# Carrying a running phase from chunk to chunk by one row, and storing a row of decays turned: linear attention with an FFN on one Trainium2 core

## The chip, the cores and the metric

One NeuronCore of a Trainium2 chip runs the whole program. The metric is the device time of one execution in microseconds. Times of one kernel mostly agree within 1%; a run over 1.5% above the fastest of its kernel is called slow and left out of every comparison. Medians and ranges below count all runs of a kernel, slow ones too; ratios use fast runs alone. The kernel before takes 300.9 us (median of four runs, 299.94 to 301.81).

The profiles name the engines in short. PE is TensorE, which multiplies matrices, and PEld its weight loads; DVE is VectorE, ACT ScalarE, POOL GpSimd. SP or SPq is SyncE, which issues most of the DMAs. PSUM is the memory into which PE writes its products. The granted clock is the share of full speed at which PE was let run. A line of waits, such as `a <- b: 57.8, 9, 18.1`, says that `a` waited for `b` for 57.8 us in all, 9 times, at the longest 18.1 us.

## The reference, cut to what matters

```python
# q, k, v, a_re, a_im: (batch 4, heads 8, seq 768, dim 48), fp32
mag = np.sqrt(a_re * a_re + a_im * a_im)
scale = np.minimum(mag, 0.999) / (mag + 1e-06)
a_re_n, a_im_n = (a_re * scale, a_im * scale)
for t in range(S):                       # complex decay of a 48x48 state per head
    new_re = ar * S_re - ai * S_im
    new_im = ar * S_im + ai * S_re
    S_re, S_im = (new_re + kv, new_im)   # kv = outer(k[t], v[t])
    y[:, :, t] = np.einsum('bhd,bhde->bhe', q[:, :, t], S_re)
# then, on the 3072 x 384 tokens x made of y:
out = sigmoid(x @ w_gate) * (x @ w_val) @ w_out      # d_ff 1536
```

A product of complex decays is a product of sizes and a sum of angles. The kernel cuts each batch's 768 steps into 6 chunks of 128 (24 chunks in all). In a chunk, a triangular matmul turns per-step log sizes into cumulative decays and per-step angles into cumulative phases. Only a phase modulo 2π matters, but it must contain the angles of all the earlier chunks of the same batch. How that carry is made is one subject of the change; the other is how the row of a chunk's total decays is stored.

## The kernel before

Every piece of work is a named step for a chunk `m` or a group `g` of one to three chunks. Lists of numbers, `TIMES`, are sorted to give each engine its fixed order. The parts that matter here:

```python
# total decay of a chunk: row 127 of EE, one row of 384 floats, to DRAM ...
nc.sync.dma_start(scr[b][c:c + 1], T[EE][L - 1:L, 0])                    # step scr
# ... and back as 48 partitions x 8 heads, for the chunks lo..hi of a group
nc.sync.dma_start(rbe[b][p0:p0 + D, lo:hi],
                  scr[b][lo:hi].rearrange("c (h d) -> d c h", d=D))      # step rbe, p0 = 0, 64
# DVE needs it before it can pass the state on
nc.vector.tensor_tensor(out=arr[b][:, c], in0=rbe[b][:, c - 1],
                        in1=rbe[b][:, c], op=ALU.mult)
# [...]
# phase of a chunk, in turns; A[:, 1, s] holds arctan, 128 x 384 fp32
nc.tensor.matmul(ct, wt_t, T[A][:, 1, s], start=True, stop=False)        # step ct
if prev:                                                                 # earlier chunks
    nc.tensor.matmul(ct, on_t, T[prev[0]], start=False, stop=False)      # the ones-matmul
# step run, on POOL: RUN = previous RUN + this chunk's angles
nc.gpsimd.tensor_tensor(out=T[RUN], in0=T[prev[0]], in1=th, op=ALU.add)
# step r16 on DVE rounds ct to an integer, step nid on PE subtracts it:
nc.tensor.matmul(T[CT][:, :HD], nid_t, T[R16], start=False, stop=True)
# step cs on ACT: Abs and two Sin of ct, which give cosine and sine
```

`wt_t` is the triangle over 2π, `on_t` a full matrix of 1/(2π), both fp32.

Of the kernel before, what the change touches and what calls it, by code (L numbers as in the profile page):

```python
# [25 lines left out]

BRISK = 1
# [3 lines left out]
        1.6, 5.95],  # L31
    "wg": [
        9.61, 19.75, 36.31],
    "wv": [
        14.45, 28.31, 41.72],
    "wo": [
        47.02, 54.23, 60.97],
    "la": [
        0.7, 5.05, 11.4, 23.58, 30.23, 40.45, 49.35, 57.89, 62.4, 67.84,
        74.04, 81.04, 87.55, 98.44, 105.44, 109.79, 122.19, 127.84,  # L40
        135.59, 150.82, 155.17, 160.92, 191.36, 199.88],
    "sq": [
        5.05, 16.5, 38.15, 55.66, 73.64, 94.11, 116.4, 140.2, 168.36,
        212.24],
    "add": [
        5.92, 18, 21.03, 39.65, 40.74, 57.78, 58.87, 75.78, 76.87,
        78.36, 96.26, 97.34, 100.63, 119.7, 120.79, 122.39, 142.35,
        147.63, 150.71, 173.29, 174.38, 175.97, 213.75, 214.83],
    "min": [
        6.52, 20.52, 22.74, 42.49, 43, 60.46, 59.95, 79.84, 80.35,  # L50
        80.86, 100.12, 102.74, 101.71, 125.67, 121.87, 126.18, 151.69,
        148.72, 152.2, 176.95, 175.46, 181.85, 215.81, 216.32],
    "lna": [
        7.31, 19.12, 44.34, 60.42, 80.37, 105.13, 129.27, 158.34,
        187.78, 216.56],
    "lnm": [
        6.93, 23.36, 43.64, 61.12, 81.49, 104.12, 128.25, 157.32,
        186.77, 217.26],
    "inv": [
        9.73, 19.99, 48.13, 61.82, 82.88, 106.53, 131.29, 159.73,  # L60
        188.97, 217.95],
    "r": [
        10.76, 23.25, 24.23, 49.97, 48.99, 64.17, 62.69, 86.02, 85.04,
        84.07, 107.71, 108.69, 109.66, 132.48, 133.45, 134.43, 161.89,
        162.87, 160.92, 192.62, 191.13, 190.16, 219.8, 218.82],
    "cl": [
        7.48, 27.36, 24.23, 44.59, 45.88, 61.99, 62.63, 83.42, 84.06,
        85.15, 106.64, 107.28, 108.37, 130.32, 129.68, 131.61, 158.99,
        160.56, 161.2, 188.31, 190.46, 188.95, 218.82, 218.18],
    "ee": [  # L70
        8.97, 28.86, 25.72, 46.09, 47.37, 62.84, 63.6, 84.65, 85.41,
        86.17, 107.92, 108.68, 109.44, 132.31, 130.53, 133.06, 160.75,
        161.51, 162.26, 190.74, 191.5, 189.99, 219.79, 219.03],
    "scr": [
        31.13, 29.78, 26.65, 47.01, 48.3, 64.65, 68.74, 88.45, 88.9,
        87.1, 115.04, 110.69, 114.59, 134.89, 134.44, 133.99, 169.43,
        169.88, 168.98, 192.88, 192.43, 190.91, 220.72, 223.91],
    "rbe": [
        38.2, 35.85, 50.55, 71.34, 80.09, 93.19, 121.29, 120.39, 136.99,
        171.98, 198.06, 195.81, 226.56],  # L80
    "lq": [
        2.95, 12.3, 22.23, 27.8, 39.1, 51.45, 63.3, 72.69, 78.74, 84.49,
        90.74, 96.64, 106.34, 113.24, 119.04, 124.54, 138.34, 144.92,
        151.72, 158.62, 170.33, 175.83, 181.33, 196.71],
    "v16": [
        9.1, 22.23, 27.8, 35.8, 67.46, 63.66, 81.38, 79.33, 88.79,
        91.11, 111.66, 110.64, 116.37, 144.3, 125.16, 146.61, 147.12,
        165.65, 169.45, 172.27, 227.38, 181.33, 186.83, 235.3],
    "qke": [
        9.9, 29.78, 31.58, 55, 50.95, 65.15, 71.29, 86.99, 89.31, 98.32,  # L90
        114.57, 117.9, 123.36, 138.92, 144.81, 135.91, 170.47, 167.64,
        163.85, 193.59, 195.39, 197.2, 223.78, 225.58],
    "atan": [
        11.4, 30.9, 51.06, 65.64, 88.76, 112.41, 136.76, 164.69, 195.44,
        221.84],
    "ct": [
        12.06, 33.89, 37.44, 51.92, 54.71, 66.55, 69.24, 90.06, 92.74,
        94.35, 115.66, 119.6, 121.21, 138.43, 140.37, 144.63, 168.26,
        171.08, 178.77, 198.7, 201.88, 203.65, 222.8, 226.31],
    "run": [  # L100
        18.98, 33.38, 37.08, 53.26, 56.8, 73.09, 91.62, 92.7, 94.23,
        113.59, 117.39, 137.95, 143.32, 149.74, 166.16, 172.78, 199,
        200.2, 203.37, 222.8],
    "r16": [
        13.55, 36.67, 38.93, 53.42, 56.2, 68.05, 70.09, 91.55, 94.88,
        96.54, 117.81, 121.54, 123.53, 141.01, 142.2, 146.64, 169.76,
        172.57, 179.89, 200.2, 203.37, 205.17, 224.29, 227.8],
    "nid": [
        14.16, 37.28, 39.54, 54.02, 56.81, 68.7, 70.93, 92.2, 95.96,
        98.03, 118.53, 122.18, 124.13, 141.65, 143.01, 147.33, 170.92,  # L110
        176.68, 180.79, 201.18, 205.42, 207.04, 225.01, 228.64],
    "cs": [
        14.69, 39.48, 40.75, 54.39, 57.37, 69.46, 71.37, 92.57, 96.98,
        98.52, 118.9, 123.2, 124.74, 142.18, 144.67, 147.7, 171.51,
        177.06, 182.07, 201.55, 206.01, 207.41, 225.38, 229.01],
    "ks": [
        16.13, 40.92, 42.79, 56.91, 60.91, 70.89, 79.74, 94.01, 99.19,
        104.49, 120.34, 126.78, 131.07, 143.61, 150.45, 153.44, 173.04,
        180.35, 184.16, 203.84, 207.83, 217.73, 226.82, 230.45],
    "qs": [  # L120
        17.13, 41.93, 45.62, 58.18, 62.37, 72.09, 80.75, 95.34, 103.29,
        109.17, 122.33, 129.6, 132.5, 145.31, 155.5, 158.59, 177.63,
        181.9, 192.63, 205.63, 211.28, 218.74, 228.27, 235.25],
    "tp": [
        18.14, 19.02, 43.37, 42.93, 48.3, 47.6, 59.19, 61.45, 63.37,
        64.46, 73.86, 73.09, 86.11, 84.7, 97.26, 96.49, 105.22, 107.92,
        111.6, 112.53, 124.64, 123.34, 132.9, 134.23, 136.45, 143.7,
        146.4, 148.03, 160.12, 161.84, 162.77, 163.7, 182.18, 184.51,
        193.49, 185.44, 196.42, 206.11, 210.03, 213.06, 215.55, 219.63,
        220.78, 221.87, 230.84, 231.77, 240.92, 239.29],  # L130
    "qkT": [
        19.23, 21.22, 45.02, 44.42, 49.39, 48.79, 59.84, 63.23, 64.16,
        65.12, 75.08, 74.15, 87.2, 85.36, 97.93, 97.33, 107.49, 108.58,
        112.25, 113.78, 125.29, 123.99, 133.56, 134.88, 137.61, 147.1,
        148.17, 148.76, 160.77, 162.5, 163.43, 165.33, 182.83, 186.11,
        194.14, 187.74, 197.07, 206.77, 210.68, 213.94, 216.21, 220.28,
        223.58, 222.52, 233.02, 232.42, 242.33, 241.74],
    "sc": [
        19.97, 21.96, 47.16, 47.38, 50.78, 54.49, 60.58, 65.45, 65.23,
        72, 75.89, 76.44, 88.13, 87.05, 99.64, 100.19, 110.18, 111.05,  # L140
        114.03, 114.58, 127.03, 126.48, 134.67, 135.74, 142.3, 148.96,
        149.66, 150.37, 164.14, 164.59, 164.37, 173.5, 183.8, 190.24,
        197.35, 193.93, 200.47, 207.74, 212.35, 214.68, 220.56, 224.79,
        229.29, 224.08, 237.88, 240.21, 243.43, 244.14],
    "mst": [
        20.62, 22.61, 47.59, 48.19, 51.81, 54.92, 61.77, 66.88, 66.28,
        72.95, 77.62, 78.22, 88.99, 87.8, 100.07, 101.9, 110.61, 111.48,
        116.2, 115.01, 130.47, 128.54, 135.48, 136.55, 142.73, 149.39,
        151.78, 152.38, 168.4, 167.8, 165.92, 174.37, 185.02, 190.67,
        198.73, 198.14, 201.86, 209.09, 213.34, 215.54, 220.99, 226.06,  # L150
        231.31, 225.46, 238.31, 241.14, 243.86, 244.73],
    "kv": [
        30.6, 49.33, 49.69, 57.92, 68.16, 87.6, 100.73, 102.34, 109.66,
        125.95, 134.9, 151.08, 155.44, 157, 177.38, 191.75, 213.98,
        230.16, 232.21, 237.19],
    "P": [
        31.21, 49.98, 53.88, 60.44, 68.57, 92.02, 102.5, 106.32, 110.07,
        129.14, 136.08, 154.31, 158.13, 160.16, 178.49, 192.16, 216.8,
        231.91, 234.79, 239.38],
    "y": [  # L160
        23.35, 48.93, 56.16, 70.2, 75.17, 79.13, 91.67, 102.88, 113.3,
        117.8, 133.35, 137.55, 151.77, 153.17, 170.03, 179.9, 191.95,
        209.14, 210.96, 217.78, 228.24, 236.3, 242.55, 245.54],
    "y16": [
        26.48, 50.45, 56.99, 70.99, 75.89, 82.5, 92.1, 106.15, 113.91,
        118.41, 133.96, 138.16, 152.18, 153.78, 175.44, 180.51, 194.31,
        209.75, 211.37, 218.65, 230.74, 236.91, 245.44, 254.09],
    "xp": [
        27.03, 51.17, 57.54, 72.55, 76.99, 86.56, 101.27, 112.04,
        115.12, 119.07, 137.38, 140.2, 154.05, 156.14, 175.99, 181.48,  # L170
        208.45, 211.65, 214.9, 219.46, 238.59, 241.85, 249.83, 258.91],
    "xt": [
        27.57, 51.55, 57.92, 73.88, 78.81, 86.93, 105.35, 113.18,
        115.94, 119.44, 138.79, 141.47, 154.77, 157.86, 177.36, 183.89,
        208.82, 212.14, 215.28, 219.84, 239.84, 244.46, 261.67, 261.94],
    "pg": [
# [744 lines left out]
```

## Time and profile before

| | before |
|---|---|
| median time | 300.9 us |
| span of the profiled run, mean granted clock | 300.8 us, 0.977 |
| PE stream, by my sum | 235.8 us |
| PE stalls in the first 80 us / after | 41.4 / 12.9 us |

PE's stream and stalls come from the start-to-start spacings of PE's instructions in the trace. For each shape the shortest usual spacing is its stream; whatever is above it is a stall, half-clock time included. Stream and stalls leave 10.7 us before the first and after the last matmul.

### The profile page before, as it was taken

What the parts mean: (1) busy time and instruction counts of PE and PEld (TensorE: products, weight loads), DVE (VectorE), ACT (ScalarE), POOL (GpSimd) and SP (SyncE); (2) the same over time, 40 slices, a digit from 0 to 9 for tenths busy, and PEclk for the clock granted to TensorE, in tenths of its full rate; (3) what the DMA queues carried; (4) which work ended last, traced back from release to release, by engine and by line L of the source; (5) the groups of instructions that cost most, each with busy time, mean ns of one, the idle gap of its engine ahead of it and who ended that gap; (6) DMA issues with size and microseconds to landing.
All of it is one profiled execution on the core that took longest, in us unless ns stands there. A gap on an engine that the chain in (4) does not pass through costs nothing.

```text
span 300.8 us, 6265 instructions
## 1 busy us (share of the span) xinstructions
PE 258.9 (86%) x2328; PEld 177.2 (59%) x2328; DVE 212.2 (71%) x389; ACT 208.9 (69%) x368; POOL 161.9 (54%) x173
## 2 busy tenths in 40 slices
PE   0443668649999998998999999999999999999995
PEld 0131446436675675866766666566667666766683
DVE  3251268978993699879889976994699889825340
ACT  3663777838978988978996798579668963334341
POOL 0327684966466894898579579727733642100000
PEclk9999987978999999999999999999999999999999
DMA  7999999996793999829392795743820011001011
GB/s 147 171 180 148 183 127 205 128 181 121 147 176 56 158 181 163 143 20 218 55 188 42 129 187 118 135 71 75 142 49 2 26 3 56 1 28 52 26 54 52
DMA packets 152030, 32.69 MB, mean 109 GB/s; under 512 B 144552, under 2 KB 152000, under 8 KB 152000
## 3 DMA queue, kind: packets, MB, share of 16 engines
q1 hardware_dynamic: 148016, 28.76, 54.5%
q0 software_dynamic: 3984, 3.54, 8.3%
q8 instruction: 18, 0.29, 0.4%
q14 instruction: 12, 0.10, 0.1%
HBM read 31.07 MB, written 4.76 MB: 119 GB/s over the span
## 4 chain that ended last, share of the span: by engine, by line
PE 38%; DVE 15%; POOL 14%; issue 10%; ACT 7%; SPq 7%; DMA 7%; DVEq 0%; POOLq 0%; ACTq 0%
PE o L862 10%; PE v L832 8%; PE g L832 8%; SPq L473 4%; POOL lm L514 4%; POOL lm L522 4%; PE cl L556 4%; DVE arr L743 3%; DVE p L848 3%; POOL qk L606 2%; DMA rbe<-scr 2%; DMA a<-in_a_re_dram 2%; DVE mst L729 2%; PE sc L722 2%; DVE kst L676 2%
## 5 line engine op out<-in xcount | busy, mean ns | idle before, releaser
L842 ACT ACTIVATE g<-g 128x384 f16<-128x384 f32 (+2 forms) x120 | 49.1, 427 | 39.1 <-PE g L832 36.9
L848 DVE SCALAR_TENSOR_TENSOR p<-g,v 128x384 f16<-128x384 f16 (+2 forms) x120 | 54.9, 467 | 26.4 <-ACT g L842 12.3
L832 PE MATMUL g<-xt,wg 128*128 128x384 f16 (+2 forms) x360 | 67.7, 298 | 5.0 <-ACT g L842 4.4
L832 PE MATMUL v<-xt,wv 128*128 128x384 f16 (+2 forms) x360 | 67.8, 298 | 0.3 <-DVE p L848 0.2
L862 PE MATMUL o<-wo,p 128*128 128x384 f16 x288 | 56.5, 328 | 0.0
L832 PEld LDWEIGHTS <-wg 128*128 128x128 f16 x360 | 32.3, 99 | 20.4 <-issue 10.0
L606 POOL TENSOR_TENSOR qk<-qk,ee 128x768 f32<-128x768 f32 x23 | 42.3, 1846 | 3.6 <-ACT ee L564 3.3
L832 PEld LDWEIGHTS <-wv 128*128 128x128 f16 x360 | 32.8, 100 | 15.8 <-issue 4.7
L550 POOL TENSOR_TENSOR a<-a 128x384 f32<-128x384 f32 x23 | 25.8, 1143 | 30.2 <-ACT a L540 25.1
L714 DVE COPY qkT<-tp 128x1024 f16<-128x1024 f16 x48 | 32.4, 685 | 12.1 <-PE tp L706 12.0
L514 POOL TENSOR_TENSOR lm<-sq 128x384 f32<-128x384 f32 x23 | 24.9, 1094 | 25.6 <-ACT sq L506 25.3
L887 ACT ACT_TABLE_LOAD x29 | 37.2, 1283 | 0.5
L862 PEld LDWEIGHTS <-p 128*128 128x128 f16 x288 | 27.4, 98 | 16.7 <-issue 1.7
L729 DVE TENSOR_TENSOR mst<-sc,msk_t 128x512 f16<-128x512 f32 x48 | 32.2, 683 | 5.9 <-PE sc L722 5.8
L556 PE MATMUL cl<-lm,wl_t 128*128 128x384 f32 x48 | 22.9, 588 | 11.6 <-ACT lm L535 11.1
L705 PE MATMUL tp<-idn_t,kst 128*128 128x128 f16 x192 | 28.8, 229 | 2.5 <-DVE kst L676 2.5
L676 DVE TENSOR_TENSOR kst<-qk,cs 128x768 f16<-128x768 f32 x24 | 26.8, 1117 | 4.9 <-ACT cs L668 2.9
L706 PE MATMUL tp<-idn_t,qst 128*128 128x128 f16 x192 | 28.3, 229 | 1.6 <-DVE qst L676 1.4
L624 PE MATMUL ct<-a,wt_t 128*128 128x384 f32 x48 | 20.9, 517 | 3.7 <-ACT a L612 3.7
L676 DVE TENSOR_TENSOR qst<-qk,cs 128x768 f16<-128x768 f32 x24 | 23.9, 997 | 0.0
L705 PEld LDWEIGHTS <-kst 128*128 128x128 f16 x192 | 19.7, 103 | 6.7 <-DVE kst L676 4.3
L706 PEld LDWEIGHTS <-qst 128*128 128x128 f16 x192 | 19.6, 103 | 5.6 <-DVE qst L676 2.7
(55 smaller groups left out, 432.7 us busy)
## 6 DMA issues: line engine op xcount, KB each, us to landing
a<-in_a_re_dram SPq DMA_DIRECT2D x24, 192.0 KB
a<-in_a_im_dram SPq DMA_DIRECT2D x24, 192.0 KB
qk<-in_k_dram SPq DMA_DIRECT2D x24, 192.0 KB
qk<-in_q_dram SPq DMA_DIRECT2D x24, 192.0 KB
v<-in_v_dram SPq DMA_DIRECT2D x24, 192.0 KB
out_dram<-ot SPq DMA_DIRECT2D x24, 192.0 KB
wg<-in_moe_w_gate_dram POOLq DMA_DIRECT2D x3, 384.0 KB, 7.0
wv<-in_moe_w_val_dram POOLq DMA_DIRECT2D x3, 384.0 KB, 5.5
```

The lines of the kernel that those rows point to most:

```text
L514: eng(g).tensor_tensor(out=T[LM][:, s], in0=T[SQ][:, 0, s], in1=T[SQ][:, 1, s], op=ALU.add)
L556: nc.tensor.matmul(T[CL][:, :HD], wl_t, T[LM][:, s], start=True, stop=True)
L606: eng(g).tensor_tensor(out=T[QK], in0=T[QK], in1=T[EE], op=ALU.mult)
L676: nc.vector.tensor_tensor(out=T[SL][i].rearrange("p h (r x) -> p h r x", r=2)[:, :, :, 0:D], in0=heads(T[QK][:, i]).unsqueeze(2) .broadcas ...
L705: nc.tensor.transpose(tp[:, 4 + i], ks[:, h], idn_t)
L706: nc.tensor.transpose(tp[:, i], qs[:, h], idn_t)
L729: nc.vector.tensor_tensor(out=T[MS], in0=T[SC], in1=msk_t.unsqueeze(1).broadcast_to([L, 4, L]), op=ALU.mult)
L832: nc.tensor.matmul(T[ACC][:, :nt], w[:, j, fb * 128:fb * 128 + 128], T[XT][:, j, :nt], start=(j == 0), stop=(j == 2))
L842: nc.scalar.activation(out=T[G16][:, :nt], in_=T[PG][:, :nt], func=FT.Tanh, scale=0.5)
L848: nc.vector.scalar_tensor_tensor(out=T[PT][:, fb, :nt], in0=T[G16][:, :nt], scalar=1.0, op0=ALU.add, in1=T[PV][:, :nt], op1=ALU.mult)
L862: nc.tensor.matmul(T[PO][:, :DM], T[PT][:, fb, s * L:(s + 1) * L], wo16[:, fb], start=(fb == 0), stop=(fb == NFB - 1))
L887: nc.scalar.preload_act_table_set(SETS[key[1]])
```

## The change

The intent: the ones-matmul makes the same row, the sum over all earlier steps, 128 times over, at the price of an fp32 product. In batches 1 to 3, 15 times, row 127 of the wrapped phase of chunk m−1 is itself the carry. ACT copies the rows 96 to 127 out of PSUM, scaled so that only row 127 counts (times 2π); a GpSimd DMA moves that row to partition 0; DVE adds it to row 0 of the next chunk's angles, and the triangular matmul spreads it over all rows. I call copy, DMA and add a *link*. The ones-matmuls and POOL's running sums of these batches go. Beside that, the row of decays is turned before it is stored, so that the load back can take 32 bytes at a time, and all step times were made anew.

```diff
+ROLL = 1
 TIMES = { [all lists new; "cr", "hop", "cy" added] }
-                nc.sync.dma_start(scr[b][c:c + 1], T[EE][L - 1:L, 0])
+                with nc.allow_non_contiguous_dma(reason="row turned by heads"):
+                    nc.sync.dma_start(
+                        scr[b][c].rearrange("(d h) -> h d", h=H).unsqueeze(0),
+                        heads(T[EE][L - 1:L, 0]))
-                            scr[b][lo:hi].rearrange("c (h d) -> d c h", d=D))
+                            scr[b][lo:hi].rearrange("c (d h) -> d c h", h=H))
 [...]
+            if rolled and c:                       # rolled = b >= ROLL
+                    nc.vector.tensor_tensor(
+                        out=T[A][:1, 1, s], in0=T[A][:1, 1, s], in1=T[CD],
+                        op=ALU.add)
-            if c < NCH - 1:                        # running sum on POOL
+            if c < NCH - 1 and not rolled:
 [...]
+            if rolled and c < NCH - 1:
+                    nc.scalar.activation(
+                        out=T[CR][END], in_=T[CT][END, :HD], func=FT.Copy,
+                        scale=lst_t[END])
+                    nc.gpsimd.dma_start(T[CD], T[CR][L - 1:L])
```

## The prediction

> **What bounds the kernel now.** I read the page's busy shares and slices first, then three stretches of the span by engine, then the chain that ended last, then the groups by shape, and at the end the waits. One core runs, and the three timed runs agree within 0.5% (299.94 to 301.54 us).
>
> ```profile
> PE 258.9 (86%) x2328; PEld 177.2 (59%) x2328; DVE 212.2 (71%) x389; ACT 208.9 (69%) x368; POOL 161.9 (54%) x173
> PE   0443668649999998998999999999999999999995
> DVE  3251268978993699879889976994699889825340
> PEclk9999987978999999999999999999999999999999
> DMA  7999999996793999829392795743820011001011
> ```
>
> The slices show two kernels in one. Up to about 80 us TensorE (PE) has holes while the DMA queues are full; from there to the end it is at 9 in nearly every slice.
>
> ```profile
> 0.00:80.00 80.00, 47.01 (x376) 31.20 (x376) 46.32 (x85) 51.37 (x85) 45.78 (x57) 0.91 0.98 156
> 80.00:240.00 160.00, 154.43 (x1471) 106.99 (x1467) 132.91 (x241) 132.63 (x230) 109.39 (x110) 1.00 0.65 112
> 240.00:301.00 61.00, 57.41 (x493) 38.97 (x490) 33.00 (x65) 24.91 (x55) 6.71 (x7) 1.00 0.12 37
> ```
>
> The columns are the stretch, then PE, weight loads, VectorE (DVE), ScalarE (ACT), GpSimd (POOL), the granted clock and the DMA share. In 80 to 240 us PE is busy for 154.4 of 160 us, but DVE and ACT are at 83% each: PE leads, and two engines are close behind. After 240 us PE is alone, and the chain of waits ends in nothing but its matmuls:
>
> ```profile
> 288.65 0.65 PE o L862 x4
> 293.56 3.91 PE o L862 x24
> ```
>
> A busy PE could still be a PE that waits inside a group, so I looked at the timeline of the part that the change touches:
>
> ```profile
> 238.41 0.91 PE L624 MATMUL ct<-a,wt_t 128*128 128x384 f32 x2
> 239.16 0.81 PE L627 MATMUL ct<-run,on_t 128*128 128x384 f32 x2
> 239.81 0.39 PE L722 MATMUL sc<-qkT 128*128 128x128 f16 x4
> ```
>
> From the start of the ones-matmul to the start of the next group is 0.65 us (239.16 to 239.81), so each costs PE 0.65 us of stream, though the group table calls one of its two passes 486 ns. Adding up the start-to-start spacings above the shortest for each shape, PE loses only some 14 us to waits after 80 us, against some 58 us before.
>
> **What the Trainium skill says.** "FP8 and Floating Point Precision", TensorE Precision Notes, gives true FP32 as four passes through the array. The trace agrees: four f16 matmuls of 384 columns take 0.65 us in the chain (0.16 each), as long as this one fp32 product. "VectorE: DVE Perf Modes", in the section on the TRN2 errata, gives (N+151)/0.96 ns for an fp32 tensor_tensor of N elements per partition, so 557 ns for 384; the one full-height add on DVE took exactly that (next fence), and the rows are not in the formula. A one-row add is therefore no cheaper. "DMA: Bandwidth & Descriptors", Anatomy of one DMA (SWDGE path), gives a fixed cost of about 2.0 us for a GpSimd-issued DMA, mostly the write's receipt. The trace has no DMA of one row from POOL; the instruction alone holds POOL for 0.8 us in the weight loads, and the DMA records show their first packets 1.2 to 2.4 us after it starts when no earlier load is still draining. "TensorE: Matmul & The Clock Gate", What's actually happening, says that the array falls to half rate after an idle window of about 3.4 us. Here two stretches ran at 0.5 (42.7 to 49.5 and 63.2 to 70.0 us), both in the front.
>
> **The change part by part.** The kernel works through 24 chunks, six for each of four batches. Batch 0 keeps the old path. In batches 1 to 3 there are 15 links from one chunk to the next. Rows used for the sizes:
>
> ```profile
> L627 PE MATMUL ct<-run,on_t 128*128 128x384 f32 x40 | 16.2, 486 | 0.0
> L640 POOL TENSOR_TENSOR run<-run,a 128x384 f32<-128x384 f32 x16 | 16.8, 1050 | 3.7 <-PE ct L627 2.3 <-ACT a L612 1.0
> L659 PE MATMUL ct<-r,nid_t 128*128 128x384 f16 x24 | 8.1, 337 | 8.0 <-DVE r L652 7.9
> L665 ACT ACTIVATE cs<-ct 128x384 f32<-128x384 f32 x24 | 11.7, 489 | 10.9 <-PE ct L659 10.8
> L514 DVE TENSOR_TENSOR lm<-sq 128x384 f32<-128x384 f32 x1 | 0.6, 557 | 3.2 <-ACT sq L506 3.2
> L456 POOL DMA_DIRECT2D wg<-in_moe_w_gate_dram x3 | 2.6, 863 | 0.1
> ```
>
> PE: 15 of 20 ones-matmuls go, 15 x 0.65 = 9.7 us, nearly all of it after 80 us, where PE has little slack. Nothing is added; the warm-up matmuls in the diff have an empty list.
> POOL: 12 running sums of 1.05 us and 3 copies of 0.5 us go, 14.1 us; 15 DMA issues of 0.8 us come, 12.0 us. About even, but POOL now stops in its order for the row that ACT copies.
> DVE: 15 one-row adds of 0.557 us, +8.4 us.
> ACT: 15 copies of 32 rows from PSUM, 384 elements each as in the absolute value at L665, so 0.49 us, +7.4 us.
> DMA: 15 transfers of 1.5 KB are nothing. The row of decays is turned before it is stored: per chunk 384 stores of 4 B and 96 loads of 32 B in place of one store and 768 loads of 4 B, in all 11,520 pieces for some 18,450 of the 152,030. It helps the crowded front a little; I allow 1 us at most.
>
> The new wait matters more than the new work. Before, a chunk's phase needed only the sum of angles, which POOL could make ahead. Now chunk m+1 cannot start until chunk m's wrapped phase exists. From the end of the rounding on DVE: wrapping matmul 0.34, row copy 0.49, DMA issue to landing about 2.5 to 3.5 (estimate: the 0.8 us of issue lies inside it, the skill's 2.0 us and the 1.2 to 2.4 us to a first packet set its scale), semaphores 0.2: 3.5 to 4.5 us. What DVE has standing between that rounding and the one-row add in the order of the built program, priced with the trace's durations, is more than 12 us at the six links that cross into another group, so they are covered. At the nine links inside a group it is 4.0, 5.0, 5.4, 6.5, 4.4, 5.9, 4.7, 5.3 and 2.2 us. At 3.5 us only the last link waits, 1.3 us; at 4.5 us the waits are 0.5, 0.1 and 2.3 us; at 5.5 us, under DMA load, they sum to 1.5+0.5+0.1+1.1+0.8+0.2+3.3 = 7.5 us. I take about 3 us.
>
> Sum: DVE gets 8.4 + 3 = 11.4 us more and ACT 7.4 us more, in a stretch where each has 27 us free, and most of that free time is itself waiting in order. If the stretch shrank by its whole 9 us to 151 us, with some 14 of the 15 links in it, DVE would stand at (132.9 + 14 x 0.56) / 151 = 93%, ACT at (132.6 + 14 x 0.49) / 151 = 92%, PE at (154.4 - 9.1) / 151 = 96%. Three engines in fixed order above 90% don't interleave that well. I charge a quarter of DVE's and ACT's additions, (11.4 + 7.4) / 4 = 4.7 us, as new stalls of PE. That gives -9.7 + 4.7 = -5.0, and with 0.7 us taken off for orders that were tuned without this machine's real waits, about -4.3 us: 296.0 us. The quarter and the 0.7 are judgement, not measurement.
>
> **The rivals.** First, PE is all that counts: the whole 9.7 us comes off, 290.6 us (-3.2%). For it: PE's 14 us of waits in 220, and a last 60 us that only PE fills. Against: the DVE and ACT shares just worked out. Second, the row's journey takes the place of the matmul: if issue to landing is over 4.5 us under load, DVE waits more than 7 us at the one-row adds, everything ordered behind them slips, PE starves, and nothing or less is left, 299 to 306 us. For it: DMA is at 0.65 in the stretch and full in single slices, and the waits show that DVE already depends on such a landing:
>
> ```profile
> DVE qkT L714 <- PE tp L706: 8.4, 9, 3.7
> DVE r L652 <- PE ct L627: 3.1, 4, 1.1
> DVE arr L743 <- DMA rbe<-scr: 1.6, 3, 0.7
> ```
>
> Against: those transfers stand in SyncE's queue behind large loads, the row goes by GpSimd's queue. Third, the front decides: all step times are new, in the front too, and PE loses 58 us there. A better or worse front moves the end by 3 us either way with nothing to do with the phase, and a half-clock stretch gained or lost is worth up to 3.4 us (6.8 us at half speed).
>
> **How the range follows.** The full gain with a 1.5 us better front is 289; the lost gain with a worse front is 303. I give 289.5 to 303 eight times in ten. Faster by over 2% means below 294.3 us, 1.7 us under my number: 0.36. Slower by over 2% means above 306.3 us and needs both the long journey and a bad front: 0.06. Within 2%: 0.58.
>
> **What would show it.** Right: 10 ones-matmul records remain of 40; PE's busy time falls by about 10 us; DVE's rises by about 8 and ACT's by about 7; each one-row add takes near 0.55 us plus a visible wait at links inside a group; issue to landing is 2.5 to 3.5 us; PE's waits after 80 us grow from 14 to some 19 us. Wrong: if those waits don't grow, the first rival holds. If the one-row adds, or what stands behind them, wait for over 7 us in all, the second does. If PE's position in its work at 80 us has moved by more than 2 us, the front does. Since a wait can be recorded inside an instruction's own duration (the small multiply of decays at L743 has a median of 0.16 us and a longest of 4.28), the durations must be read as well as the list of waits.

## More of the kernel before

The prediction does not show three views. The first is the chain of waits by engine, the second the waits of SyncE, which issues most DMAs in order (total us, times, longest us), the third a piece of SyncE's timeline:

```profile
PE 38%; DVE 15%; POOL 14%; issue 10%; ACT 7%; SPq 7%; DMA 7%; DVEq 0%; POOLq 0%; ACTq 0%
```

```profile
SPq L570 <- ACT ee L562: 57.8, 9, 18.1
SPq L578 <- DMA scr<-ee: 3.8, 4, 1.2
```

L570 is the store of the row of decays, L578 the load that brings it back. SyncE waits long for ACT to make the row, and hardly at all (3.8 us in the whole run) for the store to land. Around these two lines SyncE's timeline looks like this (start, duration, what, how many):

```profile
183.25 0.87 SPq L570 DMA_DIRECT2D scr<-ee  x3
184.22 0.40 SPq L473 DMA_DIRECT2D qk<-in_k_dram  x1
184.98 0.92 SPq L473 DMA_DIRECT2D qk<-in_q_dram  x1
185.96 0.65 SPq L473 DMA_DIRECT2D v<-in_v_dram  x1
186.73 1.40 SPq L578 DMA_DIRECT2D rbe<-scr  x2
```

Three loads fill the time in which the store lands, and the read-back follows with no gap.

## The result, and the profile after

| | before | after |
|---|---|---|
| median time (lowest to highest) | 300.92 us (299.94 to 301.81) | 358.70 us (355.90 to 365.16) |
| ratio of fast runs, 95% interval | | 1.189 (1.176 to 1.202) |
| profiled span, clock | 300.8 us, 0.977 | 354.4 us, 0.918 |
| PE stream | 235.8 us | 226.1 us |
| PE stalls before / after 80 us | 41.4 / 12.9 us | 48.5 / 68.9 us |

A ratio here and below is the mean time of one kernel's fast runs over the mean of the other's from the same rounds, so it is not quite the ratio of the medians quoted. A point is a hundredth of the kernel before, some 3 us. Each ratio has its interval, of 0.4 to 1.3 points either way, so a difference of two ratios is uncertain by about 0.6 points (2 us) or more. The record holds no check of the results of these two runs; the new phase with the old store, and the old phase with the turned store, were both checked and correct.

The table already is the whole account: the stream fell by 9.7 us (by construction, as it is the number of matmuls times a fixed spacing), the stalls grew by 63.1 us, and the span is 53.6 us longer (0.2 us are at the ends). The page of the changed kernel, busy times and two rows of slices:

```profile
PE 269.6 (76%) x2298; PEld 181.2 (51%) x2298; DVE 226.2 (64%) x405; ACT 219.7 (62%) x383; POOL 156.6 (44%) x173
PE   1274758637859769886987799399679895899995
PEclk9999969867969969998999999879969999799999
```

Thirty matmul records went (15 products of two records each), and yet PE is busy for 269.6 us where it was 258.9. That is no contradiction: PE now has holes all along, the granted clock dips to 6 or 7 in slices where it had been at 9, and a matmul lasts longer on average (the mean of the FFN's gate matmuls `g` is 315 ns where it was 298). Busy time is no measure of work here; the stream is.

The stretches by engine (PE, weight loads, DVE, ACT, POOL, clock, DMA share, GB/s):

```profile
0.00:80.00 80.00, 43.22 (x316) 29.21 (x317) 39.35 (x76) 42.39 (x68) 36.34 (x46) 0.90 0.80 128
80.00:240.00 160.00, 128.09 (x1161) 86.98 (x1160) 114.53 (x204) 116.56 (x202) 92.81 (x99) 0.91 0.64 116
```

In the middle 160 us, PE gets through 1161 matmuls where it had done 1471. DVE, ACT and POOL are all less busy too. Since no engine got fuller and all got emptier, I looked for a latency rather than for an engine. The chain of waits names one, first its shares by engine and line, then a piece of it in order of time (start, duration, what):

```profile
PE 32%; DMA 25%; issue 13%; ACT 11%; POOL 6%; DVE 6%; SPq 6%; POOLq 0%; ACTq 0%; DVEq 0%
DMA scr<-ee 9%; PE v L881 7%; PE g L881 7%; DMA a<-in_a_re_dram 6%; PE o L911 6%; DMA a<-in_a_im_dram 5%; SPq L493 3%; PE cl L577 3%; PE ct L657 3%; DMA out_dram<-ot 3%; POOL lm L535 3%; DVE qst L725 2%; ACT g L891 1%; ACT L936 1%; DVE kst L725 1%
```

```profile
176.12 0.49 ACT ee L583
...
176.64 9.19 DMA scr<-ee
...
186.34 2.63 DMA rbe<-scr
```

DMA went from 7% to 25% of the chain, and its costliest line is a store of 1.5 KB. Here it takes 9.19 us from issue to landing. SyncE's waits and its timeline at the same place:

```profile
SPq L592 <- ACT ee L585: 56.7, 11, 28.2
SPq L602 <- DMA scr<-ee: 37.8, 7, 8.4
```

```profile
174.21 3.06 SPq L592 DMA_DIRECT2D scr<-ee  x3
177.32 0.50 SPq L493 DMA_DIRECT2D a<-in_a_re_dram  x1
177.88 1.19 SPq L493 DMA_DIRECT2D a<-in_a_im_dram  x1
185.95 0.82 SPq L602 DMA_DIRECT2D rbe<-scr  x2
186.82 0.44 SPq L493 DMA_DIRECT2D qk<-in_k_dram  x1
```

The wait for ACT is as before; the wait for the store's landing is ten times as long (3.8 to 37.8 us). SyncE stands from 179.1 to 185.9 us, and the loads of q, k and v in its order stand with it. The waits of DVE show the other end of the same store, and beside it the link, as the groups do:

```profile
DVE arr L792 <- DMA rbe<-scr: 24.0, 5, 6.4
...
DVE a L648 <- DMA cd<-cr: 11.6, 5, 3.7
```

```profile
L648 DVE TENSOR_TENSOR a<-a,cd 1x384 f32<-1x384 f32 x15 | 13.3, 884 | 13.1 <-DMA cd<-cr 11.6 <-ACT a L636 1.4
L700 ACT ACTIVATE cr<-ct,lst_t 32x384 f32<-32x384 f32 x15 | 8.6, 572 | 9.1 <-PE ct L692 8.8
L708 POOL DMA_DIRECT2D cd<-cr x15 | 8.5, 567 | 37.9 <-ACT cr L700 37.1 <-PE v L881 0.6
```

The link is suspicious as well: DVE stands 11.6 us for the rows (five times), and POOL 37.1 us for ACT's copies. Reading on from the longest wait would settle on one of the three without proof. So the experiments began with one part alone.

### The profile page after: what moved, and what is told of

The parts are those of the page before. It is cut to its first block, busy times and chain, and to the rows that moved or that the text cites. A ratio compares the mean times of both kernels' runs of the same rounds, so it can differ in the third digit from the quotient of the medians.

```text
span 354.4 us, 6280 instructions
## 1 busy us (share of the span) xinstructions
PE 269.6 (76%) x2298; PEld 181.2 (51%) x2298; DVE 226.2 (64%) x405; ACT 219.7 (62%) x383; POOL 156.6 (44%) x173
## 2 busy tenths in 40 slices
DMA packets 145886, 32.72 MB, mean 92 GB/s; under 512 B 138432, under 2 KB 145856, under 8 KB 145856
## 4 chain that ended last, share of the span: by engine, by line
PE 32%; DMA 25%; issue 13%; ACT 11%; POOL 6%; DVE 6%; SPq 6%; POOLq 0%; ACTq 0%; DVEq 0%
DMA scr<-ee 9%; PE v L881 7%; PE g L881 7%; DMA a<-in_a_re_dram 6%; PE o L911 6%; DMA a<-in_a_im_dram 5%; SPq L493 3%; PE cl L577 3%; PE ct L657 3%; DMA out_dram<-ot 3%; POOL lm L535 3%; DVE qst L725 2%; ACT g L891 1%; ACT L936 1%; DVE kst L725 1%
## 5 line engine op out<-in xcount | busy, mean ns | idle before, releaser
L881 PE MATMUL g<-xt,wg 128*128 128x384 f16 (+2 forms) x360 | 72.8, 315 | 12.9 <-ACT g L891 8.0
L881 PE MATMUL v<-xt,wv 128*128 128x384 f16 (+2 forms) x360 | 71.4, 311 | 10.6 <-ACT ot L921 7.3
L881 PEld LDWEIGHTS <-wg 128*128 128x128 f16 x360 | 34.7, 104 | 31.1 <-issue 20.7
L881 PEld LDWEIGHTS <-wv 128*128 128x128 f16 x360 | 34.8, 104 | 28.8 <-issue 17.5
L657 PE MATMUL ct<-a,wt_t 128*128 128x384 f32 x48 | 25.3, 614 | 17.0 <-issue 12.5
L754 PE MATMUL tp<-idn_t,kst 128*128 128x128 f16 x192 | 31.2, 243 | 8.5 <-DVE kst L725 7.9
L527 ACT ACTIVATE sq<-a 128x2304 f32<-128x2304 f32 (+2 forms) x10 | 17.4, 1738 | 31.6 <-issue 17.4
L755 PE MATMUL tp<-idn_t,qst 128*128 128x128 f16 x192 | 30.4, 243 | 7.9 <-DVE qst L725 7.8
L725 DVE TENSOR_TENSOR kst<-qk,cs 128x768 f16<-128x768 f32 x24 | 28.4, 1182 | 4.5 <-ACT cs L717 2.0
L725 DVE TENSOR_TENSOR qst<-qk,cs 128x768 f16<-128x768 f32 x24 | 30.0, 1252 | 0.0
```

The costliest lines, as they stand in the source:

```text
L725: nc.vector.tensor_tensor(out=T[SL][i].rearrange("p h (r x) -> p h r x", r=2)[:, :, :, 0:D], in0=heads(T[QK][:, i]).unsqueeze(2) .broadcas ...
L755: nc.tensor.transpose(tp[:, i], qs[:, h], idn_t)
L881: nc.tensor.matmul(T[ACC][:, :nt], w[:, j, fb * 128:fb * 128 + 128], T[XT][:, j, :nt], start=(j == 0), stop=(j == 2))
```

## The experiments

Four theories were on the table. *Store*: the turned store of the decays is what costs. *Landing*: the link's row arrives late, and everything ordered behind it slips. *Work*: the link's instructions on DVE, ACT and POOL crowd engines that had no room. *Order*: the new step times are worse by themselves. Where a kernel gives a wrong result I say so; all others were correct. The expectations give a range for each theory. In six runs the result fell outside all of them by more than the noise: the flat store in the new kernel, the turned store in the old one, every second element, 64 bytes each, the new order alone, and six links by POOL. I then went by the nearer range, or by the difference to another run.

### Each suspect alone

**The new kernel with the old store and load of the decays** (called `row_flat`; many later kernels start from it).

```diff
-                    nc.sync.dma_start(
-                        scr[b][c].rearrange("(d h) -> h d", h=H).unsqueeze(0),
-                        heads(T[EE][L - 1:L, 0]))
+                nc.sync.dma_start(scr[b][c:c + 1], T[EE][L - 1:L, 0])
-                            scr[b][lo:hi].rearrange("c (d h) -> d c h", h=H))
+                            scr[b][lo:hi].rearrange("c (h d) -> d c h", d=D))
```

> The changed kernel with the row of decays stored as before: one contiguous 1.5 KB store, read back in 768 loads of 4 B per chunk. Theory D (the turned store, 384 pieces of 4 B into DRAM, lands 6 to 8 us late, and SyncE stands still for it with all loads behind it): 293 to 301 us, SyncE's wait for the store falls from 37.8 us to under 6. Theory H (the one-row DMA of the phase holds the chain): still 345 to 360 us. Theory O (the new order of steps is bad in itself, whatever the DMA): still 345 to 360 us.

Measured: 311.26 us median, ratio 1.0318 (1.0265 to 1.0371). SyncE's wait for the store, and the middle stretch:

```profile
SPq L599 <- DMA scr<-ee: 1.2, 1, 1.2
```

```profile
80.00:240.00 160.00, 142.10 (x1360) 95.95 (x1358) 140.54 (x242) 132.01 (x229) 103.65 (x107) 1.00 0.57 110
```

Taking the turned store out of the new kernel gives back 15.7 points of the 18.9, some 47 us, and the clock of the stretch is back at 1.00. The rest, 3.2%, is still a loss, and belongs to something else: PE's stalls after 80 us are 30.3 us, against 12.9 before.

**The old kernel with the turned store and load** (the same edit the other way round).

> The kernel before with nothing changed but the turned store and its turned read. Theory D: 325 to 360 us, with SyncE waiting over 25 us for the store to land (3.8 before). Theories H and O: 299 to 302 us, as before, since phase and order are those of before.

Measured: 381.72 us, ratio 1.2628 (1.2539 to 1.2717); clock 0.892. In the old order the store alone costs 79 us, more than the whole change does. So the store is both enough for the loss, and needed for most of it. ("The store" is here the turned store with the load that fits it; they were always changed together. In the changed kernel's chain the store took 9.19 us to land and the load 2.63.)

```profile
SPq L581 <- DMA scr<-ee: 44.6, 8, 8.7
```

```profile
DVE arr L746 <- DMA rbe<-scr: 43.1, 7, 9.9
```

**The new kernel, where the row's DMA still goes, but the add reads a row of zeros and waits for nothing** (wrong), once with the turned store and once with the flat one.

```diff
-                        out=T[A][:1, 1, s], in0=T[A][:1, 1, s], in1=T[CD],
+                        out=T[A][:1, 1, s], in0=T[A][:1, 1, s], in1=nil,
-                    use=[A, f"cd_{m - 1}"])
+                    use=[A])
```

> The changed kernel, turned store kept; the one-row DMA still goes, but the one-row add reads a constant row of zeros and waits for no DMA (the result is wrong on purpose). Theory D: 340 to 358 us, little gained. Theory H: 295 to 305 us. Theory O: 345 to 358 us.

> Contiguous store and no wait for the one-row DMA (wrong result on purpose). It measures what the journey of the row costs once the store is out of the way. Theory D alone, with the journey hidden as the prediction had it: 0 to 5 us below row_flat. If the journey was under-sized too: 6 to 15 us below row_flat.

Measured: 358.73 us, 1.1904 (1.1835 to 1.1973), with the turned store: the same as with the waits (1.189). With the flat store 308.53 us, 1.0265 (1.020 to 1.033), against 1.0318: 0.5 points or 1.6 us, with intervals that overlap. *Landing* falls as the main cause: the 11.6 us that DVE is seen to stand for the row cost nothing that could be measured beside the store, and without the store the difference is too small to be resolved. The DMA view of the row's tile in the changed kernel, then in `row_flat`, shows that the row's journey is also shorter where the store is flat:

```profile
DMA to landing us min/median/max: 1.5/3.1/6.5
```

```profile
DMA to landing us min/median/max: 1.5/2.0/4.2
```

**The row's DMA issued by ACT right behind its own copy**, in place of POOL, which stands 37.1 us for the copies in the changed kernel and 22.6 us in `row_flat`.

```diff
-                    nc.gpsimd.dma_start(T[CD], T[CR][L - 1:L])
+                    nc.scalar.dma_start(T[CD], T[CR][L - 1:L])
```

> row_flat with the one-row DMA issued from ACT's queue right behind the copy that makes the row, so that POOL waits for nothing of it. If POOL standing at the DMA issue (22.6 us of waiting for the row copy in row_flat) holds others up: 1.00 to 1.02 of before. If that wait of POOL costs nothing: 1.03 to 1.035, like row_flat.

Measured: 310.79 us, 1.0316 (1.0259 to 1.0373), the same as `row_flat`. No net cost of POOL's wait is seen. It is a net result: ACT now issues the DMAs, and in the kernels with six links below that cost 1.7 points, so a gain on POOL may be hidden in it. The 37.1 us beside the turned store were not tested.

### What in the store costs

A turned store differs from a flat one in more than one way: 384 pieces of 4 bytes in place of one row, and pieces that lie next to each other in DRAM come from different heads. Two stores in the old kernel and the old order take these apart.

**Every second element**: still 384 pieces of 4 bytes, in the old order of elements, each beside a gap of 4 bytes.

```diff
-    scr = [dram.tile([NCH, HD], F32, ...)]
+    scr = [dram.tile([NCH, HD, 2], F32, ...)]
-                nc.sync.dma_start(scr[b][c:c + 1], T[EE][L - 1:L, 0])
+                    nc.sync.dma_start(
+                        scr[b][c, :, 0].rearrange("(h d) -> h d", h=H).unsqueeze(0),
+                        heads(T[EE][L - 1:L, 0]))
```

> The kernel before, the row of decays stored in its old order but into every second element of the scratch, so in 384 pieces of 4 B, none next to another; read in 768 pieces of 4 B as before. If the pieces of the store are the cost: 1.20 to 1.30 of before, like the turned store (1.263). If it was the turned order or the 32 B read: 0.99 to 1.02.

Measured: 342.10 us, 1.1319 (1.1232 to 1.1407). The page gives the store's median time from issue to landing (last number):

```profile
scr<-ee SPq DMA_DIRECT2D x24, 1.5 KB, 6.9
```

Pieces without turning do about half of the harm, so turning isn't needed for a loss. At that point "the number of pieces" looked like the cause, with the turning as an addition.

**Every element on 64 bytes of its own**: turned, again 384 pieces of 4 bytes; the load back has 768 pieces of 4 bytes, as in the kernel before.

```diff
-    scr = [dram.tile([NCH, HD], F32, ...)]
+    scr = [dram.tile([D, NCH * H, 16], F32, ...)]
-                nc.sync.dma_start(scr[b][c:c + 1], T[EE][L - 1:L, 0])
+                    nc.sync.dma_start(
+                        scr[b][:, c * H:(c + 1) * H, 0]
+                        .rearrange("d h -> h d").unsqueeze(0),
+                        heads(T[EE][L - 1:L, 0]))
```

> The kernel before, the row of decays stored turned by heads as in the change, but each element on its own 64 B of the scratch, so that no two DMA engines write into the same 64 B; read in 768 pieces of 4 B. If engines sharing the same few bytes is what doubles the cost of the turned store: 1.10 to 1.16 of before, like the spaced one (1.132). If distance between an engine's own pieces is: 1.22 to 1.30, like the turned one (1.263).

Measured: 313.36 us, 1.0385 (1.0314 to 1.0455), far below both ranges that I had expected. The profiled run was a slow one (316.4 us), so I use its waits for their size only:

```profile
SPq L582 <- DMA scr<-ee: 8.6, 7, 2.8
```

The theory of the number falls. With the same 384 pieces of the same 4 bytes, from the same heads in the same turned order, the loss is 3.9% in place of 26.3% when the pieces lie apart. (The loads back differ as well, but the padded kernel has the worse one, 768 pieces of 4 bytes where the turned one has 96 of 32, so they don't explain it.) The four kernels of the old order side by side:

| store of 384 floats | its floats in 64 bytes of DRAM | SyncE waits for landing, us (longest) | DVE waits for the load back, us | median us | ratio |
|---|---|---|---|---|---|
| one row (before) | 16, one piece | 3.8 (1.2) | 1.6 | 300.9 | 1 |
| padded | 1 | 8.6 (2.8) | 10.5 | 313.4 | 1.039 |
| every second | 8, from one head | 22.2 (4.5) | 34.4 | 342.1 | 1.132 |
| turned | 16, from eight heads | 44.6 (8.7) | 43.1 | 381.7 | 1.263 |

So what costs is separate small stores that lie close together in DRAM. That closeness matters, and not the number alone, is shown by the padded store against the turned one. The four kernels also stand in the order of closeness, but between the spaced and the turned store the order of the heads changes too, so the steps of that order are not shown one by one. Not shown either: over what distance (64 bytes is only my unit; 32 would order the four the same way, and as the padded row is spread over 48 stretches of 3,072 bytes, a longer one is possible too), whether it matters that neighbours come from different heads, and how much of the time is lost by SyncE standing (loads late) or by DVE standing for the load back. Both waits grow together.

The packet records of the same traces show a third path. The loads of a, q, k and v move 122,880 packets of 192 bytes in each kernel. Of these, 34 took over 0.3 us in the kernel before, 44 with the padded store, 228 with every second element and 293 with the turned store (39 in `row_flat`, 256 in the changed kernel). So loads that are already under way are slowed too. In the changed kernel, SyncE had issued two loads of `a` by 179.1 us. Until the store landed at 185.8 us little moved, and then much (the last two numbers are the DMA share and GB/s):

```profile
178.00:186.00 8.00, 6.78 (x70) 4.48 (x68) 7.98 (x14) 5.58 (x10) 6.59 (x7) 1.00 0.26 23
186.00:190.00 4.00, 3.10 (x35) 1.87 (x33) 2.28 (x5) 3.67 (x7) 0.57 (x1) 1.00 0.85 152
```

Why the loads crawl beside such a store, and how much of the 47 us this is, no run shows.

### What the other three per cent are made of

**The new order alone**: `row_flat` with the old phase in all batches, so no link; four buffers for the running sum.

```diff
-ROLL = 1
+ROLL = 4
 TIMES: [running sums of batches 1 to 3 put in; cr, hop, cy out]
-    t_run = kind("run", 2, [L, HD], F32)
+    t_run = kind("run", 4, [L, HD], F32)
```

> The new step times with the phase carried as before (ones-matmuls and running sums; four buffers for the sums so that POOL isn't held) and the contiguous store. row_flat measured 1.032 of before, with the new phase. Theory R (what is left is the price of the links: POOL stopped at the DMA issue, extra DVE and ACT work): 0.99 to 1.005 of before. Theory O (what is left is the new order itself): 1.03 to 1.07, since 9.7 us of matmul come back on top.

Measured: 305.53 us, 1.0183 (1.0124 to 1.0243). The order costs 1.8%, with the reservation that it was made for a kernel with links, and that I placed the sums in it by hand (with two buffers for them the program could not be built without a deadlock).

**No links, and no sums or ones-matmuls either**: `row_flat` without copy, DMA and add (wrong).

```diff
-            if rolled and c:
+            if rolled and c and False:
-            if rolled and c < NCH - 1:
+            if rolled and c < NCH - 1 and False:
```

> row_flat with row copy, DMA and one-row add all left out in batches 1 to 3 (wrong result on purpose): the new order with the ones-matmuls gone and nothing in their place, the most that taking them away could give in this order. Theory R: 0.96 to 0.985 of before, 15 to 20 us under row_flat. Theory O: 1.01 to 1.03.

Measured: 295.35 us, 0.9823 (0.9765 to 0.9881). Against the order alone, that is 3.6 points: what removing the old carry is worth in this order, 10.8 us.

**Only the add** (of zeros, behind the previous chunk's wrapping matmul; no copy, no DMA), and **only copy and DMA** (no add); both wrong.

```diff
 only the add:
-                        out=T[A][:1, 1, s], in0=T[A][:1, 1, s], in1=T[CD],
+                        out=T[A][:1, 1, s], in0=T[A][:1, 1, s], in1=nil,
-            if rolled and c < NCH - 1:
+            if rolled and c < NCH - 1 and False:
 only copy and DMA:
-            if rolled and c:
+            if rolled and c and False:
```

> row_flat without row copy and DMA, the one-row add left in with a constant row of zeros (wrong result on purpose). no_links measured 0.982 of before, flat_nohop (all links' work, no wait for the landing) 1.0265. If the add on DVE, which now stands between arctangent and phase matmul, is the dear part: 1.01 to 1.025. If the copy on ACT and the issue are: 0.985 to 1.0.

> row_flat without the one-row add, row copy and DMA left in (wrong result on purpose). If the add is the dear part: 0.985 to 1.0. If the copy on ACT (0.57 us each, ahead of cosine and sine) is: 1.01 to 1.025.

Measured: 301.38 us, 1.0007 (0.9967 to 1.0047), and 302.30 us, 1.0038 (0.9991 to 1.0084). Over the kernel with neither (0.9823), the adds cost 1.84 points or 5.5 us, copy and issue 2.15 points or 6.5 us, and both without the wait for landing 4.42 points or 13.3 us (1.0265 of the kernel above with zeros and the flat store). The groups of the two in the kernel with zeros and the flat store:

```profile
L647 DVE TENSOR_TENSOR a<-a,nil 1x384 f32<-1x384 f32 x15 | 12.3, 821 | 1.7 <-ACT a L635 1.6
L699 ACT ACTIVATE cr<-ct,lst_t 32x384 f32<-32x384 f32 x15 | 8.6, 572 | 3.8 <-PE ct L691 3.5
```

*Work* holds: of the 20.9 us that the link takes on DVE and ACT, 13.3 us are paid, about two thirds. The median add takes 0.546 us, but some last up to 1.67 us, though they wait for no row; what lengthens those is not known. The copies also make ACT wait 3.5 us for the wrapping matmul. The experiments do not separate the work from such waits that its place in the order brings.

**The ones-matmuls out, the sums kept; the sums out, ones-matmuls of zeros kept**, both on the new order alone, both wrong.

```diff
 no ones-matmuls:
-                if prev:
+                if prev and b < 1:
 no sums:
+                elif more:
+                    nc.tensor.matmul(ct, on_t, nil, start=False, ...)
-            if c < NCH - 1 and not rolled:
+            if c < NCH - 1 and b < 1:
```

> order_only (new order, old phase, 1.018 of before) with the 15 ones-matmuls of batches 1 to 3 left out and the sums on POOL kept (wrong result on purpose). If PE's 9.7 us are the gain seen in no_links (0.982): 0.98 to 0.995 of before. If the sums are: 1.005 to 1.02.

> order_only with the sums on POOL left out in batches 1 to 3 and the ones-matmuls kept on a constant tile of zeros, so that they wait for nothing (wrong result on purpose). If PE's 9.7 us are the gain: 1.01 to 1.02 of before. If the sums are: 0.985 to 1.0.

Measured: 299.75 us, 0.9958 (0.9906 to 1.001), and 303.00 us, 1.0055 (1.0003 to 1.0107). From 1.0183, the ones-matmuls are worth 2.25 points or 6.8 us of PE's 9.7, the sums 1.28 points or 3.9 us. The two add up to the 3.6 points found above.

### Is there a cheaper carry?

**A link only where a new group begins** (six in place of 15), ones-matmuls inside a group, in the old order; the row's DMA issued by ACT, then by POOL.

```diff
+            into = rolled and c and s == 0
+            out_of = rolled and c < NCH - 1 and s == n - 1
+            prev = None if rolled and s == 0 else last_run.get(b)
 [add if into; copy and DMA if out_of, as in the change]
 second kernel:
-                    nc.scalar.dma_start(T[CD], T[CR][L - 1:L])
+                    nc.gpsimd.dma_start(T[CD], T[CR][L - 1:L])
```

> The order of before, contiguous store; the one-row DMA only at the six links that cross from one group to the next, where over 12 us of other work lie between; inside a group the ones-matmul stays. It takes away 6 ones-matmuls (6 x 0.65 = 3.9 us of PE) and 9 us of POOL's sums for 6 x 0.56 us of DVE and 6 x 0.6 us of ACT. Theory R and theory O both: 0.985 to 1.0 of before, if the links are as well hidden as the prediction had it. Above 1.01: links cost even where they have room.

> cross_scalar with its six DMAs issued by GpSimd as in the change; cross_scalar had 1.031 in its timed runs, and a profile with TensorE at half speed throughout, which can't be read. If ACT's issue of the DMA was what cost: 0.985 to 1.005. If the copy and the add themselves cost, or this order lost its fit: 1.02 to 1.04, as hop_act was no slower than row_flat.

Measured: 310.76 us (the median of six runs, with the slow one described next), 1.0311 (1.0262 to 1.0361), and 305.36 us, 1.0137 (1.0078 to 1.0196). Both lose. That the issuing engine makes 1.7 points here and none in `row_flat` I cannot explain: the profiled run of the first took 526.8 us with its matmuls at about half speed (the records of its fp32 matmuls start 665 ns apart, not 322), so its trace is no use, and its five other runs were fast.

**The same sum in fp16**: running sum and ones matrix as fp16, so the 20 ones-matmuls need one pass. Old order.

```diff
-        np.full((L, L), 1.0 / TWO_PI, np.float32), name="glk_on")
+        np.full((L, L), 1.0 / TWO_PI, np.float16), name="glk_on")
-    t_run = kind("run", 2, [L, HD], F32)
+    t_run = kind("run", 2, [L, HD], F16)
```

> The kernel before with the running sum and the ones-matrix in fp16 instead of fp32: all 20 ones-matmuls stay, in one pass of 0.16 us instead of 0.65, and nothing is added or waits. 20 x 0.485 = 9.7 us less for PE, some 7.3 us of it after 80 us. If PE's time in this order is worth what it was worth in the new one (15 ones-matmuls, 9.7 us: order_only to no_links 10.2 us): 0.965 to 0.98 of before, and faster than both kernels. If the order of before is held by something else: 0.985 to 1.0.

Measured: 299.63 us, 0.9963 (0.9912 to 1.0015): not the hoped gain but the second case of the expectation. Most of what PE saves does not reach the end. The middle stretch, and the group of the ones-matmul, now with one matmul record each:

```profile
80.00:240.00 160.00, 149.61 (x1446) 103.07 (x1444) 132.46 (x241) 132.16 (x227) 111.20 (x112) 1.00 0.64 110
```

```profile
L627 PE MATMUL ct<-run,on_t 128*128 128x384 f16 x20 | 6.7, 335 | 0.0
```

PE is less busy in the stretch (149.6 for 154.4 us), while DVE and ACT do what they did before: in the old order these 160 us are not set by PE alone. By my sums the stalls after 80 us grew from 12.9 to 19.2 us.

**The sums out in the old order** (zeros for the ones-matmuls, wrong; the edit is that of the no-sums kernel above).

> The same in the order of before: ones-matmuls of batches 1 to 3 on zeros, no sums (wrong result on purpose). If POOL's 14 us or the wait for them hold this order (where sum_f16 showed PE's time to be worth 0.4%): 0.965 to 0.985. If neither does, and orders this tight just fill up elsewhere: 0.99 to 1.0.

Measured: 299.43 us, 0.9944 (0.9896 to 0.9993). POOL's sums and copies are worth 0.6%, about 1.7 us of the 14.1 us that they take.

**Angles in fp16, no sums at all**: ACT writes the arctan as fp16 to a tile that lives on for the batch, both weight matrices are fp16, and each chunk adds one single-pass ones-matmul per earlier chunk of its batch. All four batches, old order.

```diff
+        TH = t_th(g)                              # [L, NS, HD] fp16, 5 buffers
-            nc.scalar.activation(out=T[A][:, 1, :n], in_=T[A][:, 1, :n],
+            nc.scalar.activation(out=T[TH][:, :n], in_=T[A][:, 1, :n],
                                  func=FT.Arctan)
-                if prev:
-                    nc.tensor.matmul(ct, on_t, T[prev[0]], start=False, ...)
+                for p, i in prev:
+                    nc.tensor.matmul(ct, on_t, T[p][:, i], start=False, ...)
-            [step run]
```

> The order of before; arctangent written in fp16 to a tile of its own, all sums over time in fp16 with one pass of 0.16 us: the cumulative matmul 24 x 0.485 = 11.6 us cheaper, the carry as one fp16 ones-matmul per earlier chunk of the batch (60 x 0.16 = 9.7 us in place of 20 x 0.65 = 13), no running sums on POOL (18.8 us less), nothing added on DVE or ACT. PE is 14.9 us lighter. If sums or matmuls are worth their time: 0.94 to 0.975 of before. If, as in sum_f16, the room just turns into other waits: 0.985 to 1.0. The rounding of the angles to fp16 should stay within what the result allows.

Measured: 295.84 us, 0.9814 (0.9774 to 0.9853), correct. It beats both kernels: 1.9% under the kernel before, about 17% under the changed one. The gain is small beside what left PE (14.9 us of stream) and POOL (16 sums and 4 copies, 18.8 us); stalls after 80 us grew to 22.8 us.

## Why the prediction was wrong, point by point

The prediction was 296.0 us, with a range to 303; it was 358.7. Written as a sum, with the parts measured on top of each other (points of the ratio, times 301 us):

| term | predicted us | measured us | from |
|---|---|---|---|
| new order | 0.7 as a reserve; front ±3 | +5.5 | order alone |
| ones-matmuls out | −9.7 | −6.8 | order alone with and without |
| running sums out, POOL | about even with the issues | −3.9 | the same |
| work of the link | +4.0, a quarter of 15.8 | +13.3, of 20.9 | no links to links on zeros |
| waits for the row | +0.75, a quarter of 3 | +1.6, not resolved | zeros to real rows |
| turned store | −1 at most, not in the sum | +47 | flat to turned store |
| sum | −4.3 | +57 | |

The reserve was counted as a loss, so −9.7 + 4.7 + 0.7 gives the predicted −4.3. The measured terms give 56.7, and the ratio of 1.189 gives 56.9; this is no check, since each measured term but the split of ones-matmuls and sums is the difference between one kernel of the series and the next.

**The step that failed** is the one on DMA: "The row of decays is turned before it is stored: per chunk 384 stores of 4 B and 96 loads of 32 B in place of one store and 768 loads of 4 B [...] It helps the crowded front a little; I allow 1 us at most." The count of pieces is about right: 6,930 packets fewer by those numbers, 6,144 by the pages (152,030 to 145,886), with the rows' own packets among the latter. The price per piece is what failed: I let a store's piece cost what a load's does and looked at the sum of all pieces, not at the time at which one store is complete, on which the load back, SyncE's later loads and DVE wait. That time was 9.19 us in the chain for 1.5 KB, and the flat store in its place gave back some 47 us. The Trainium skill, "DMA: Bandwidth & Descriptors", Specifications, could have warned me: it gives 512 bytes as the least transfer for full rate and says that below it the engine does a read-modify-write. These runs agree that the turned row is slow; but a 4-byte piece is below 512 bytes in the padded, the spaced and the turned store alike, and they cost 3.9, 13.2 and 26.3%, so the rule alone gives no size. No run here shows the read-modify-write itself.

**PE's term was right as work** (15 products of 0.65 us went) and 70% right as time. The records of the ones-matmul fell as said.

**The quarter for DVE and ACT was mis-sized.** The work was too low. A copy took 0.572 us on ACT, not 0.49 (the 15 issues on POOL took 8.5 us, less than the 12.0 predicted). The median add was as predicted where it waited for no row (0.546 us), but the 15 adds together took 12.3 to 13.6 us in the kernels that have them, not 8.4. In the changed kernel DVE was busy for 14.0 us more than before, not 8, and ACT for 10.8, not 7. And the work was paid to some two thirds, not to a quarter: in the middle stretch of `row_flat` DVE is busy for 140.5 of 160 us and PE for 142.1, so by busy time DVE is as full as PE. I had worked out 93% for DVE and still charged a quarter. Even without the store the kernel would have been at 311, outside my range.

**The journey of the row** was sized well, 2.5 to 3.5 us predicted from issue to landing and 2.0 and 3.1 us median measured. The second rival, that its wait takes the place of the matmul, fell, in spite of 11.6 us of waits at the adds, which by the prediction's own test ("over 7 us in all") would have shown it right. That test was wrong: it took a visible wait for a paid one. What each of the waits at a link cost stays open.

**The first rival**, PE is all that counts, fell too: 14.9 us less on PE with 18.8 less on POOL made 1.9%. **The third**, the front, is right in that a new order costs something by itself (5.5 us, with the reservation made above), but the place was not the front: PE's stalls before 80 us are 40.7 us in that kernel and 41.4 before (the prediction's 58 us was a miscount). The prediction's test for it would have misled here too: in the changed kernel PE had done 316 matmuls by 80 us, not 376, and its stalls there grew by 7.1 us; but in `row_flat`, with the same order of steps and the flat store, it had done 410.

**PE's waits after 80 us**, 14 to become "some 19", became 68.9 us, and 30.3 with the flat store. The half rate that the prediction cited is seen in the granted clock's fall to 0.918; it comes back to 0.967 with the flat store, so it came with that store's stalls.

What stays open is said where it arose: the distance over which small stores disturb each other, the parts of SyncE's waits, of DVE's waits and of the slowed loads in the 47 us, the exact cost of the row's landing, and the issuing engine in the kernel with six links.

## What to carry to other kernels

Price a DMA by the time at which its last byte is known to have landed, by who waits for that and what stands behind it in the issuing engine's order; the number of pieces does not tell it, and a store of 4-byte pieces that are neighbours in DRAM can cost several times one that keeps them apart; here it was cheaper to turn the row on the load than on the store. Work that was moved here from a full engine to two that were 83% busy in fixed order was paid to two thirds, so a quarter was far too little. And before believing the longest wait in a list, take away what causes it: DVE's 11.6 us of waits for the row were worth nothing measurable beside the turned store, and moving the issue away from POOL, with its 22.6 us of waits, gained nothing in `row_flat`.

## What the Trainium skill lacked or had wrong

- "DMA: Bandwidth & Descriptors" gives the 512-byte limit and other warnings against short pieces, but nothing on what they cost when they lie close together in DRAM. With 384 pieces of 4 bytes a store, one piece in each 64 bytes cost 3.9% of the run, eight 13.2% and sixteen 26.3%.
- The same page's fixed cost of about 2.0 us (Anatomy of one DMA, the GpSimd path) agrees with the one-row DMA in `row_flat` (1.5 to 4.2 us, median 2.0). It has no figure for what neighbouring small stores add: 6.9 us median for 1.5 KB with every second element, 9.19 us in the chain of the changed kernel, both issued by SyncE.
- I found on no page that an engine's standing in the order need not cost anything: DVE's 11.6 us of waits for the row in the changed kernel went with no change of the time (1.1904 for 1.189) when the add read zeros.
- On no page did I find a whole run at half PE speed under a recorded clock of 1.0. "TensorE: Matmul & The Clock Gate" comes nearest: it warns that recorded clock events can be unreliable. Here one execution took 526.8 us with a recorded clock of 1.0, where the same kernel took 308.0 to 311.2 us in its other five runs. Its cause is not known.
